# Attention's key blocks moved by 64, with the first block's low part in the free half of its high part

## The chip, the core and the metric

The kernel runs on one core of one Trainium2 chip. TensorE (PE) multiplies matrices: it loads a block of weights of up to 128x128 and streams the columns of the other operand past it, and the result goes to PSUM, which this kernel uses as eight banks of 128 partitions by 512 fp32 columns. ScalarE (ACT), VectorE (DVE) and GpSimd (POOL) do the element work, and SyncE (SP) issues the transfers. The metric is the device time of one execution in microseconds (us), the median of several runs.

## The reference

What is computed is causal attention with a decay bias, and behind it a mixture of four experts, each a two-layer network, weighted by probabilities:

```python
# q, k, v: (4, 8, 576, 64); s: (4, 8, 576)
scores = q @ k^T / 8 ; cum = cumsum(max(s, 0))
scores += min(-(cum[i] - cum[j]), 0), masked where j > i
attn = softmax(scores) ; a = attn @ v          # per head
x = a as (2304 tokens, 512)
p = domain_probs / sum(domain_probs)
out = sum over e of p[:, e] * (relu(x @ w1[e]) @ w2[e])   # 512 -> 1024 -> 512
```

A head has 576 queries and keys: 4 x 128 + 64.

## The kernel before

**Precision.** Most products are split: an operand is written as a high part, which the ACT engine rounds to fp32r, and a low part, the rest, which DVE or POOL subtracts; the products high x high, high x low and low x high are summed in PSUM.

**Attention in visits.** `VISITS` (lines 30 and 31) lists the work. The first eight visits take tiles 0, 1 and 2 of the eight heads of the first batch, the next eight their tiles 3 and 4, and 24 visits the five tiles of each remaining head. Query tile m holds the queries `rows(m)`: tile 0 the first 64, tile m the 128 from 128m - 64 on. Tile m needs the keys 0 to 128m + 64. In the 24 five-tile visits, tile 0 of two heads is done together by `pair_rows`.

For each tile the steps are: scores into a PSUM bank (lines 745 and 748), row maximum with the mask on DVE (line 759), exponential on ACT (line 767), the reciprocal of the sum on DVE (line 775), the normalisation on POOL, ACT or DVE (line 461 or 459), the transposition on PE (line 794), which turns a block of 128 queries by 128 keys so that keys lie on partitions, the high part out of PSUM into `aTh` on ACT (line 466), and the low part on DVE into `aTl` (line 823). When a visit's tiles are through, one run of matmuls with V (line 844) sums over all key blocks, first those of `aTh`, then those of `aTl`. V's high and low part stand side by side in the weights.

**Key blocks.** Block n holds the keys 128n to 128n + 127, block 4 only 64 real ones. Queries and key blocks are thus out of step by 64: a tile m reaches only half into its last block. In the visits behind the first eight, block 4 has no low part of its own. Its unused upper 64 partitions in `aTh` take it (line 826), and V's block 4 holds the last 64 rows twice. The transpositions of tile 4 are in two groups, blocks 0 and 1 in one PSUM bank and blocks 2 to 4 in another (line 783).

**Weights and moving operand of a transposition.** In line 794 the attention block is the weight operand, the identity `idn` the moving one.

**The order.** A planner (`Sched.run`) simulates the engines when the program is built, with costs such as `t_pe` and `t_dve`, priorities and lags, and writes one fixed order for each engine. Attention has the priority. Where PE has nothing of it, the planner puts in matmuls of expert 0 (lines 945 and 960, "fill-in" below) and, early on, dummy matmuls (line 486). What of expert 0 is left follows behind attention, and then come the other experts' products (line 1302), which run from some 400 us to the end.

Of the kernel before, what the change touches and what calls it, by code (L numbers as in the profile page):

```python
# [11 lines left out]
F32 = mybir.dt.float32  # L12
F32R = mybir.dt.float32r
AF = mybir.ActivationFunctionType
ALU = mybir.AluOpType
# [4 lines left out]
B, NH, S, D = 4, 8, 576, 64  # L20
BH = B * NH
E, DM, F = 4, 512, 1024
NT = B * S
P = 128
NC = 5
# [30 lines left out]
    return (0, 64) if m == 0 else (128 * m - 64, 128 * m + 64)  # L56


def fcs_of(tiles):
    return range(KF // 2, KF) if tiles[0] >= PAIRS[LG][0][0] else range(KF)  # L60


def t_pe(n):
    return max(n / 2.4 + 13.5, 110)
# [10 lines left out]
def t_dve(n):  # L75
    return n / 0.96 + 70
# [26 lines left out]
DSLACK = 1100  # L103
T_DSLACK = 15000
T_LAG = 200
S_LAG = 50
PSUM_POOLS = ("S", "T", "X", "mo", "pv")
NWARM = 7
# [30 lines left out]
PT = 0  # L139
PE_ = 0  # L140
# [192 lines left out]
                now = min(later)  # L333


def body(ctx, tc, qk, qkv0, vp, s, dp, w1, w1s, w2, w2s, out):
    nc = tc.nc
    sch = Sched()
    const = ctx.enter_context(tc.tile_pool(name="const", bufs=1))
# [10 lines left out]
    idn = apool.tile([P, P], F32, name="idn")  # L350
# [44 lines left out]
    mo = [b[1] for b in sch.pools["mo"]]  # L395
# [15 lines left out]
    aTh = apool.tile([P, 512 + 5 * 640], F32R, name="aTh")  # L411
    aTl = apool.tile([P, 512 + 5 * 640], F32R, name="aTl")
# [37 lines left out]
    tok = sch.tok  # L450
# [35 lines left out]
        nc.tensor.matmul(b[1][:, 0:256], ones_bf[:, 0:128], ones_bf[:, 0:256], start=True, stop=True)  # L486
        return 110

    for _ in range(NWARM):
        nc.tensor.matmul(mo[1], ones_bf[:, 0:128], ones_bf, start=True, stop=True)  # L490
    nc.vector.memset(warm, 0.0)
    nc.gpsimd.memset(ones, 1.0)
    nc.gpsimd.memset(minus, -1.0)
# [160 lines left out]
    for j, (h, ms) in enumerate(VISITS):  # L654
# [12 lines left out]
        if first:  # L667
            ld = sch.add({"SP": 700}, lambda e, j=j, h=h, ext=ext: nc.sync.dma_start(
                out=AB(j, F32)[0:64, :, 0:ext], in_=qk[h, :, 0:ext].rearrange("(c d) n -> d c n", c=2)),
                prio=base - 1500, take=[("AB", j)], seq="AB", xfer=128 * ext * 4)  # L670
            ldv = sch.add({"SP": 450}, lambda e, j=j, h=h, nb=nb, o=o: nc.sync.dma_start(out=tok[f"vz{h % 2}", j][:, :, o:o + 64], in_=vp[h][:, 0:nb]),
                          prio=base - 1300, take=[(f"vz{h % 2}", j)], seq=f"vz{h % 2}", xfer=nb * 128 * 64 * 4)
        else:
            if pq:
                def f(e, j=j, h=h, ext=ext, q0=q0):
                    nc.sync.dma_start(out=AB(j, F32)[0:64, 1, 0:ext], in_=qk[h, 64:128, 0:ext])
                    nc.sync.dma_start(out=AB(j, F32)[0:64, 0, q0:ext], in_=qk[h, 0:64, q0:ext])
                ld = sch.add({"SP": 800}, f, [firstq.get(j - LA)], prio=base - 1500, take=[("AB", j)], seq="AB", xfer=64 * (2 * ext - q0) * 4)
            else:
                ld = sch.add({"SP": 500}, lambda e, j=j, h=h, ext=ext: nc.sync.dma_start(out=tok["raw", j][:, 0:ext], in_=qk[h, :, 0:ext]),  # L680
                             [firstq.get(j - LA)], prio=base - 1500, take=[("raw", j)], seq="raw", xfer=128 * ext * 4)
            ldv = sch.add({"SP": 450}, lambda e, j=j, h=h, nb=nb: nc.sync.dma_start(out=tok["vraw", j][:, 0:nb], in_=vp[h][:, 0:nb]),
                          [firstq.get(j - LV)], prio=base - 1300, take=[("vraw", j)], seq="vraw", xfer=nb * 128 * 64 * 4)
        ldc = None
        if pq:
# [43 lines left out]
        for m in ms[1:] if joint else ms:  # L729
# [50 lines left out]
            nm = sch.add({"POOL": t_pool(bb), "ACT": (bb / 1.2 + 190, D1), "DVE": (t_dve2(bb), D5 if first else D6)}, f, [rc], prio=pr - PN, give=[("sm", c)])  # L780
            nm.both = True

            tp = [list(range(m + 1))] if m < 4 else [[0, 1], [2, 3, 4]]
            prev = None
            for pi, blocks in enumerate(tp):
                lastp = pi == len(tp) - 1
                w0 = 128 * blocks[0]
                w = 128 * len(blocks) if m else 64

                def f(e, m=m, j=j, blocks=blocks, c=c, pi=pi, first=first):  # L790
                    z = tok[f"a{m}", c]
                    t = tok["T", (c, pi)]
                    for k, x in enumerate(blocks[::-1] if not first and tok["par", j] else blocks):
                        nc.tensor.transpose(t[:, 128 * k:128 * k + 128], z[:, 128 * x:128 * x + 128], idn)  # L794
                tt = sch.add({"PE": t_pe(128) * len(blocks)}, f, [nm, prev, par], prio=pr - PT, take=[("T", (c, pi))],
                             give=[(f"a{m}", c)] if lastp else [])
                tt.lag = T_LAG
                prev = tt

                def region(aT, t, n0, n1, m=m, j=j, blocks=blocks, a=a, bb=bb, first=first):  # L800
                    k0 = 128 * (blocks[-1] + 1 - n1 if not first and tok["par", j] else n0 - blocks[0])
                    k = n1 - n0
                    src = t[:, k0:k0 + 128 * k].rearrange("p (k i) -> p k i", k=k)[:, :, 0:bb - a]
                    return src, tok["aTf", j][:, n0:n1, a:bb] if first else aT_blocks(aT, tok["par", j], n0, n1, a, bb)

                two = m == NC - 1 and blocks[-1] == m

                def f(e, c=c, pi=pi, region=region, blocks=blocks):
                    src, dst = region(aTh, tok["T", (c, pi)], blocks[0], blocks[-1] + 1)
                    hi(e, dst, src)  # L810
                eng = {"ACT": t_act(w)}
                if first:
                    eng["DVE"] = (t_dve(w), D4)
                eh = sch.add(eng, f, [tt], prio=pr - PE_, give=[("T", (c, pi))] if first else [])
                if first:
                    evs.append(eh)
                    continue

                def f(e, c=c, pi=pi, region=region, blocks=blocks, two=two, j=j):
                    t = tok["T", (c, pi)]  # L820
                    n0, n1 = blocks[0], blocks[-1] + 1 - two
                    (src, dst), (_, h_) = region(aTl, t, n0, n1), region(aTh, t, n0, n1)
                    nc.vector.tensor_tensor(out=dst, in0=src, in1=h_.bitcast(F32), op=ALU.subtract)  # L823
                    if two:
                        src, h_ = region(aTh, t, n1, n1 + 1)
                        nc.vector.tensor_tensor(out=h_[64:128, :, 64:128], in0=src[0:64, :, 64:128], in1=h_[0:64, :, 64:128].bitcast(F32), op=ALU.subtract)
                evs.append(sch.add({"DVE": t_dve(w) + 95 * two}, f, [eh], prio=pr - PE_, give=[("T", (c, pi))]))

        pk = ("pair", j // 2)
        pvk = ("pv", pk if first else j)  # L830
        ads = []
        for r0, r1 in ((max(cut, q0), ext),):
            mms = [(aT, n, max(r0, 128 * n), r1) for aT in (aTh, aTl)[0:1 if first else 2] for n in range(nb)
                   if max(r0, 128 * n) < r1 and not (aT is aTl and n == NC - 1)]
            bk = pvk

            def f(e, j=j, mms=mms, first=first, bk=bk, o=o, c0=cut):
                t = tok[bk]
                for i, (aT, n, i0, i1) in enumerate(mms):
                    if first:  # L840
                        st, mv = tok[f"vz{j % 2}", j][:, n, :], tok["aTf", j][:, n, i0:i1]
                    else:
                        st, mv = tok["V", j][:, n, :], aT_blocks(aT, tok["par", j], n, n + 1, i0, i1)[:, 0, :]
                    nc.tensor.matmul(t[:, i0 - c0:i1 - c0], st, mv, start=(i == 0 and not (first and o)),  # L844
                                     stop=(i == len(mms) - 1 and (not first or o > 0)))
            cost = sum(t_pe4(w - u) if first else t_pe(w - u) for _, _, u, w in mms)
            v = sch.add({"PE": cost}, f, evs + [v_ready] + ([prev_v] if first and o else []), prio=base + PO,
                        take=[bk] if not (first and o) else [], give=[(f"vz{j % 2}", j), ("aTf", j)] if first else [("V", j), ("par", j)])
            if first:
                ads.append(v)  # L850
                continue

            def f(e, j=j, o=o, r0=r0, r1=r1, pk=pk, bk=bk, c0=cut):
                nc.scalar.activation(tok["xr", pk][o:o + 64, r0:r1], tok[bk][64 - o:128 - o, r0 - c0:r1 - c0], AF.Copy)
            sh = sch.add({"ACT": t_act(r1 - r0)}, f, [v], prio=base + PO + 10, take=[("xr", pk)] if o == 0 else [])

            def f(e, j=j, o=o, r0=r0, r1=r1, pk=pk, bk=bk, c0=cut):
                xr = tok["xr", pk]
                nc.vector.tensor_tensor(out=xr[o:o + 64, r0:r1], in0=tok[bk][o:o + 64, r0 - c0:r1 - c0], in1=xr[o:o + 64, r0:r1], op=ALU.add)
            ads.append(sch.add({"DVE": t_dve(r1 - r0)}, f, [sh], prio=base + PO + 10, give=[bk]))  # L860
            if joint and o:
                ads += pair_product(j, base, [sh] + prev_ad)
# [676 lines left out]
```

## Time and profile before

| | |
|---|---|
| median of 3 runs | 914.79 us (914.31 to 914.81) |
| profiled execution | 914.74 us, its span 913.0 us |
| PE busy | 905.0 us, 99% |
| DVE busy | 705.6 us, 77% |
| ACT busy | 501.3 us, 55% |
| POOL busy | 506.4 us, 55% |
| DMA | 201.34 MB, 221 GB/s on average |

A matmul appears twice in the profile: as a weight load (PEld) and as the matmul (PE). Both overlap with their neighbours, so that the time one takes of PE is read from start to start. The ACT share is an average: while attention runs, until some 260 us, ACT is busy far above it, and after that at about 40%.

### The profile page before, as it was taken

Reading aid. Unit: us, or ns where it says so; the run is one execution under the profiler, and the core shown is the slowest. Engines: PE = TensorE matmul, PEld = TensorE weight load, DVE = VectorE, ACT = ScalarE, POOL = GpSimd, SP = SyncE. Lnnn points to the kernel's source line nnn. Section 1 sums busy time; section 2 is a strip of 40 time slices with the busy share of each in tenths; the row PEclk is TensorE's granted clock in tenths of the full one; section 3 lists DMA queues with packets and bytes.
Section 4 is the critical chain, followed back from the end, with each engine's and each line's share of the span. In section 5 each row is a group of like instructions: output and inputs, shape, how many; then the busy total and the mean of one; then the engine's idle time right before and its main releaser. Section 6 shows DMA issues by size and latency. Waiting matters only on the chain.

```text
span 913.0 us, 16499 instructions
## 1 busy us (share of the span) xinstructions
PE 905.0 (99%) x5566; PEld 879.2 (96%) x5566; DVE 705.6 (77%) x1599; ACT 501.3 (55%) x1129; POOL 506.4 (55%) x528
## 2 busy tenths in 40 slices
PE   9999999999999999999999999999999999999998
PEld 6789999899999999999999999999999999999998
DVE  6878787888861854888787788788877887787886
ACT  6898999999972334435343533444244534444343
POOL 4688787887744891055344624471366317451655
PEclk9999999999999999999999999999999999999999
DMA  6788887879626996984786468746775667756201
GB/s 165 197 246 236 225 229 219 250 194 255 181 94 221 392 382 239 357 286 173 264 286 207 161 219 303 243 158 218 252 260 200 204 215 253 256 205 220 70 18 69
DMA packets 101279, 201.34 MB, mean 221 GB/s; under 512 B 11256, under 2 KB 66620, under 8 KB 101196
## 3 DMA queue, kind: packets, MB, share of 16 engines
q1 hardware_dynamic: 101196, 200.30, 67.2%
q8 instruction: 44, 0.72, 0.3%
q14 instruction: 39, 0.32, 0.1%
HBM read 157.34 MB, written 29.05 MB: 204 GB/s over the span
## 4 chain that ended last, share of the span: by engine, by line
PE 91%; ACT 4%; DVE 2%; POOL 1%; issue 1%; DMA 1%; SPq 0%; ACTq 0%; POOLq 0%
PE pb L1302 52%; PE mo L1302 9%; PE mo L945 6%; PE mo L960 5%; PE pv L844 4%; PE pb L960 3%; PE T L794 3%; PE S L748 2%; PE pb L945 2%; PE S L745 2%; ACT a L767 1%; PE X L794 1%; ACT aTh L466 1%; DMA AB_r<-AB_r 1%; DVE aTl L823 1%
## 5 line engine op out<-in xcount | busy, mean ns | idle before, releaser
L1302 PE MATMUL pb<-x,w1h 128*128 128x384 f32 x1064 | 270.7, 335 | 0.0
L1302 PEld LDWEIGHTS pb<-x,w1h 128*128 128x128 f32 x1064 | 191.5, 188 | 2.0 <-ACT t L1335 1.5
L1302 PE MATMUL pb<-x,w1l 128*128 128x384 f32 x532 | 177.8, 334 | 0.0
L1310 ACT ACTIVATE pb<-pb 128x384 f32<-128x384 f32 x112 | 53.2, 475 | 200.5 <-DVE t L1342 111.8
L453 POOL TENSOR_TENSOR hT_r<-t,hT_r 128x768 fp32r<-128x768 f32 x18 | 34.3, 1903 | 167.8 <-PE pb L1302 139.4
L1302 PE MATMUL pb<-hT_r,w2h 128*128 128x384 f32 x432 | 109.7, 334 | 0.0
L1302 PEld LDWEIGHTS pb<-x,w1l 128*128 128x128 f32 x532 | 99.9, 188 | 0.0
L466 ACT ACTIVATE hT_r<-t 128x768 fp32r<-128x768 f32 x76 | 64.0, 843 | 47.3 <-PE pb L1302 44.3
L767 ACT ACTIVATE a<-a,mx 128x576 f32<-128x576 f32 (+4 forms) x136 | 81.0, 597 | 12.8 <-DVE mx L759 9.6
L1425 DVE TENSOR_TENSOR acc<-pb,acc 128x384 f32<-128x384 f32 x152 | 78.5, 549 | 9.6 <-ACT pb L1310 6.1
L945 PE MATMUL mo<-xg,w1h 128*128 128x384 f32 (+1 forms) x304 | 78.3, 327 | 0.0
L1302 PEld LDWEIGHTS pb<-hT_r,w2h 128*128 128x128 f32 x432 | 78.0, 188 | 0.0
L453 DVE TENSOR_TENSOR hT_r<-t,hT_r 128x768 fp32r<-128x768 f32 x58 | 59.8, 1031 | 23.2 <-ACT hT_r L466 22.7
L461 POOL TENSOR_SCALAR a<-a,sm 128x576 f32<-128x576 f32 (+5 forms) x111 | 60.5, 552 | 28.6 <-DVE sm L775 15.0
L1302 PE MATMUL pb<-xg,w2h 128*128 128x384 f32 x288 | 73.3, 335 | 0.0
L1302 PE MATMUL pb<-hT_r,w2l 128*128 128x384 f32 x216 | 72.2, 334 | 0.0
L1342 DVE TENSOR_TENSOR t<-pb,t 128x384 f32<-128x384 f32 x78 | 39.8, 551 | 38.5 <-ACT t L1335 25.6
L453 POOL TENSOR_TENSOR xg<-t,xg 128x768 fp32r<-128x768 f32 x19 | 42.9, 2259 | 40.8 <-ACT xg L466 40.8
L1070 DVE TENSOR_TENSOR t<-t 128x768 f32<-128x768 f32 (+1 forms) x42 | 65.1, 1555 | 0.1
L823 DVE TENSOR_TENSOR aTl<-T,aTh 128x256 fp32r<-128x256 f32 (+2 forms) x103 | 51.2, 508 | 4.6 <-ACT aTh L466 3.5
L759 DVE CUSTOM_DVE_ANT_0 a<-S,mask 128x448 f32<-128x448 f32 (+4 forms) x107 | 48.1, 456 | 7.5 <-PE S L745 6.1
L945 PEld LDWEIGHTS mo<-xg,w1h 128*128 128x128 f32 x304 | 52.1, 190 | 1.4 <-issue 0.7
(245 smaller groups left out, 2331.1 us busy)
## 6 DMA issues: line engine op xcount, KB each, us to landing
x<-xs_d SPq DMA_DIRECT2D x68, 768.0 KB
x<-x_d SPq DMA_DIRECT2D x55, 768.0 KB
xs_d<-x SPq DMA_DIRECT2D x12, 768.0 KB
osb<-p_d SPq DMA_DIRECT2D x19, 384.0 KB
w1r<-in_w1s_dram SPq DMA_DIRECT2D x7, 1024.0 KB
w2r<-in_w2s_dram SPq DMA_DIRECT2D x7, 1024.0 KB
KK<-AB_r SPq DMA_DIRECT2D x24, 288.0 KB
xg<-x_d SPq DMA_DIRECT2D x16, 384.0 KB
```

What stands on the lines that cost most here:

```text
L453: (nc.gpsimd if e == "POOL" else nc.vector).tensor_tensor(out=out, in0=in0, in1=in1, op=ALU.subtract)
L461: (nc.gpsimd if e == "POOL" else nc.vector).tensor_scalar(out, in_, scale, 1.0 if bias is None else bias, op0=ALU.mult, op1=ALU.mult if bi ...
L466: nc.scalar.activation(out, in_, AF.Copy)
L759: nc.vector.tensor_tensor_reduce(out=z[0:n, j0:j1], in0=tok["S", (c, pi)][0:n, 0:j1 - j0], in1=mask[0:n, 448 - a + j0:448 - a + j1], scale ...
L767: nc.scalar.activation(z[0:n, 0:bb], z[0:n, 0:bb], AF.Exp, bias=tok["mx", c][0:n, k:k + 1], scale=-1.0, accum_out=tok["sm", c][0:n])
L823: nc.vector.tensor_tensor(out=dst, in0=src, in1=h_.bitcast(F32), op=ALU.subtract)
L945: nc.tensor.matmul(t[:, 0:w], wl[q][:, dc, o:o + P], xgt[:, l, dc, 0:w], start=(u == 0), stop=(u == 3 * KD - 1))
L960: nc.tensor.matmul(t[:, 0:w], wl[fc // 2][:, fc % 2, 128 * dt:128 * dt + 128], ht[:, fc, 0:w], start=(u == 0), stop=(u == 3 * len(fcs) - 1))
L1070: (nc.gpsimd if e == "POOL" else nc.vector).tensor_tensor(out=out, in0=in0, in1=in1, op=op)
L1302: nc.tensor.matmul(ts[u], wv[wl][:, k, 128 * u:128 * u + 128], x[xl_][:, k, :], start=start and k == 0 and n == 0, stop=k == 1 and n == 2, ...
L1310: nc.scalar.activation(out[u], in_[u], AF.Copy)
L1425: nc.vector.tensor_tensor(out=d, in0=ts[u], in1=d, op=ALU.add)
```

## The change

For the visits behind the first eight, the key blocks are moved by 64: `keys(n)` gives block n the keys 128n - 64 to 128n + 63, as the query tiles are, and block 0 the first 64. Tile m then needs the blocks 0 to m in full, and it is block 0 that has 64 free partitions.

- The transposition of block 0 takes 72 columns of the attention tile as weights (64 are needed) and writes 72 partitions; it stands last in its group. Tile 4's groups become blocks 1 to 4 in one bank and block 0 in another.
- The low part of block 0 goes to the upper 64 partitions of its high part, for every tile, as a second subtraction (64x128). The other blocks' low parts are one subtraction.
- The matmuls with V have the column ranges that follow; `aTl` has no block 0.
- V comes from a new array `vd`, with the first 64 rows twice, for these visits. The first eight keep `vp`.
- The seven warm-up matmuls at the start write seven PSUM banks instead of one.
- The planner counts a group with block 0 as 40 ns shorter on PE (`T_HALF`) and the low part with two subtractions as 150 ns longer on DVE (`T_TWO`).

```diff
+def keys(n):
+    return (0, 72) if n == 0 else (128 * n - 64, 128 * n + 64)
...
+T_HALF = 40
+T_TWO = 150
...
-    for _ in range(NWARM):
-        nc.tensor.matmul(mo[1], ones_bf[:, 0:128], ones_bf, start=True, stop=True)
+    warmed = [b[1] for p in ("X", "T", "S") for b in sch.pools[p]] + mo
+    for i in range(NWARM):
+        nc.tensor.matmul(warmed[i], ones_bf[:, 0:128], ones_bf, start=True, stop=True)
...
-            ldv = sch.add({"SP": 450}, lambda e, j=j, h=h, nb=nb: nc.sync.dma_start(out=tok["vraw", j][:, 0:nb], in_=vp[h][:, 0:nb]),
+            ldv = sch.add({"SP": 450}, lambda e, j=j, h=h, nb=nb: nc.sync.dma_start(out=tok["vraw", j][:, 0:nb], in_=vd[h][:, 0:nb]),
...
-            tp = [list(range(m + 1))] if m < 4 else [[0, 1], [2, 3, 4]]
+            tp = [list(range(m + 1))] if m < 4 else [[1, 2, 3, 4], [0]]
...
-                    for k, x in enumerate(blocks[::-1] if not first and tok["par", j] else blocks):
-                        nc.tensor.transpose(t[:, 128 * k:128 * k + 128], z[:, 128 * x:128 * x + 128], idn)
-                tt = sch.add({"PE": t_pe(128) * len(blocks)}, f, [nm, prev, par], prio=pr - PT, take=[("T", (c, pi))],
+                    for k, x in sorted(enumerate(blocks[::-1] if not first and tok["par", j] else blocks), key=lambda y: not first and y[1] == 0):
+                        if first:
+                            nc.tensor.transpose(t[:, 128 * k:128 * k + 128], z[:, 128 * x:128 * x + 128], idn)
+                        else:
+                            u, w = keys(x)
+                            nc.tensor.transpose(t[0:w - u, 128 * k:128 * k + 128], z[:, u:w], idn)
+                tt = sch.add({"PE": t_pe(128) * len(blocks) - T_HALF * (not first and blocks[0] == 0)}, f, [nm, prev, par], prio=pr - PT, take=[("T", (c, pi))],
...
-                    n0, n1 = blocks[0], blocks[-1] + 1 - two
-                    (src, dst), (_, h_) = region(aTl, t, n0, n1), region(aTh, t, n0, n1)
-                    nc.vector.tensor_tensor(out=dst, in0=src, in1=h_.bitcast(F32), op=ALU.subtract)
-                    if two:
-                        src, h_ = region(aTh, t, n1, n1 + 1)
-                        nc.vector.tensor_tensor(out=h_[64:128, :, 64:128], in0=src[0:64, :, 64:128], in1=h_[0:64, :, 64:128].bitcast(F32), op=ALU.subtract)
-                evs.append(sch.add({"DVE": t_dve(w) + 95 * two}, f, [eh], prio=pr - PE_, give=[("T", (c, pi))]))
+                    n0, n1 = blocks[0] + zero, blocks[-1] + 1
+                    if n0 < n1:
+                        (src, dst), (_, h_) = region(aTl, t, n0, n1), region(aTh, t, n0, n1)
+                        nc.vector.tensor_tensor(out=dst, in0=src, in1=h_.bitcast(F32), op=ALU.subtract)
+                    if zero:
+                        src, h_ = region(aTh, t, 0, 1)
+                        nc.vector.tensor_tensor(out=h_[64:128], in0=src[0:64], in1=h_[0:64].bitcast(F32), op=ALU.subtract)
+                evs.append(sch.add({"DVE": t_dve(w) + T_TWO * (zero and m < NC - 1)}, f, [eh], prio=pr - PE_, give=[("T", (c, pi))]))
...
-            mms = [(aT, n, max(r0, 128 * n), r1) for aT in (aTh, aTl)[0:1 if first else 2] for n in range(nb)
-                   if max(r0, 128 * n) < r1 and not (aT is aTl and n == NC - 1)]
+            n0 = 128 if first else 64
+            mms = [(aT, n, max(r0, 128 * n + n0 - 128), r1) for aT in (aTh, aTl)[0:1 if first else 2] for n in range(aT is aTl, nb)
+                   if max(r0, 128 * n + n0 - 128) < r1]
...
-    vp = np.ascontiguousarray(vz.reshape(BH, NC, P, D).transpose(0, 2, 1, 3))
+    vp = np.ascontiguousarray(vz.reshape(BH, NC, P, D).transpose(0, 2, 1, 3)[0:NH])
+    vd = np.ascontiguousarray(np.concatenate([v[:, 0:64], v], 1).reshape(BH, NC, P, D).transpose(0, 2, 1, 3))
```

The lines behind the diff's first places have moved: the transposition of line 794 stands in line 804, the low parts of 823 and 826 in 834 and 837, the matmuls with V of 844 in 856, the fill-in of 945 in 957.

The first place is PE, at the tiles 2 and 3 of an early five-tile visit (tiles `a_1_124` and `a_1_126`) and the matmuls with V of the visit ahead of it. `T`, `X`, `S` and `mo` are PSUM banks; a row reads output, moving operand, weights, and the output's partitions by columns. Before:

```order
L945 MATMUL mo_103<-xg,w1h_76 128x256 x2
L844 MATMUL pv_100<-aTh,V_115 128x512
L844 MATMUL pv_100<-aTh,V_115 128x448
L844 MATMUL pv_100<-aTh,V_115 128x320
L844 MATMUL pv_100<-aTh,V_115 128x192
L844 MATMUL pv_100<-aTh,V_115 128x64
L844 MATMUL pv_100<-aTl,V_115 128x512
L844 MATMUL pv_100<-aTl,V_115 128x448
L844 MATMUL pv_100<-aTl,V_115 128x320
L844 MATMUL pv_100<-aTl,V_115 128x192
L794 MATMUL T_98<-idn,a_1_124 128x128 x3
L794 MATMUL X_101<-idn,a_1_126 128x128 x4
```

Now, for the same tiles and V:

```order
L804 MATMUL X_101<-idn,a_1_124 72x128
L957 MATMUL mo_102<-xg,w1l_80 128x256
L804 MATMUL T_99<-idn,a_1_126 128x128 x3
L804 MATMUL T_99<-idn,a_1_126 72x128
L856 MATMUL pv_100<-aTh,V_115 128x512 x2
L856 MATMUL pv_100<-aTh,V_115 128x384
L856 MATMUL pv_100<-aTh,V_115 128x256
L856 MATMUL pv_100<-aTh,V_115 128x128
L856 MATMUL pv_100<-aTl,V_115 128x512
L856 MATMUL pv_100<-aTl,V_115 128x384
L856 MATMUL pv_100<-aTl,V_115 128x256
L856 MATMUL pv_100<-aTl,V_115 128x128
```

The last transposition of each group has 72 output partitions, the matmuls with V have other columns, and the planner has put this run of them behind the next visit's transpositions instead of ahead of them.

The second place is DVE, at the low parts of the tiles 3 and 4 of a five-tile visit. Before:

```order
L823 TENSOR_TENSOR aTl<-T_99,aTh 128x4x128
L823 TENSOR_TENSOR aTl<-T_98,aTh 128x2x128
L823 TENSOR_TENSOR aTl<-X_101,aTh 128x2x128
L826 TENSOR_TENSOR aTh<-X_101,aTh 64x64
L759 ISA a_1_128,mx_140<-S_97,mask,mx_140 128x288
```

Now:

```order
L834 TENSOR_TENSOR aTl<-mo_102,aTh 128x3x128
L837 TENSOR_TENSOR aTh<-mo_102,aTh 64x128
L782 RECIPROCAL sm_146<-sm_146 128x1
L766 ISA a_1_128,mx_140<-S_96,mask,mx_140 128x288
L766 ISA mx_140 128x1
L780 TENSOR_SCALAR sm_148<-sm_148 128x1
L871 TENSOR_TENSOR cx<-pv_100,cx 64x512
L834 TENSOR_TENSOR aTl<-T_99,aTh 128x4x128
L837 TENSOR_TENSOR aTh<-X_101,aTh 64x128
```

Four subtractions stand in both places, 1,088 columns in all before and 1,152 now; each tile has its second, short one, and between the two tiles the planner has put other work.

## Rows read from the trace of the kernel before

**Rows 1.** The page's first part: busy time, share, instructions of the engines.

```profile
PE 905.0 (99%) x5566; PEld 879.2 (96%) x5566; DVE 705.6 (77%) x1599; ACT 501.3 (55%) x1129; POOL 506.4 (55%) x528
```

**Rows 2.** By stretch: length, busy PE PEld DVE ACT POOL (count), clock, DMA share, GB/s.

```profile
40.00:80.00 40.00, 40.00 (x297) 36.63 (x295) 31.63 (x112) 36.42 (x90) 33.48 (x45) 1.00 0.78 226
80.00:120.00 40.00, 39.32 (x303) 37.85 (x302) 32.75 (x136) 37.38 (x108) 32.23 (x59) 1.00 0.90 236
120.00:160.00 40.00, 39.74 (x307) 38.40 (x307) 33.41 (x129) 37.67 (x105) 32.66 (x56) 1.00 0.81 226
160.00:200.00 40.00, 38.85 (x255) 35.41 (x254) 33.87 (x136) 38.12 (x106) 33.56 (x62) 1.00 0.85 236
200.00:240.00 40.00, 40.00 (x267) 37.76 (x268) 32.40 (x132) 35.91 (x100) 31.22 (x53) 1.00 0.82 238
240.00:272.00 32.00, 32.00 (x212) 30.49 (x211) 25.45 (x90) 26.52 (x72) 17.78 (x37) 1.00 0.31 100
...
500.00:600.00 100.00, 100.00 (x577) 99.62 (x577) 78.92 (x121) 42.86 (x76) 47.89 (x29) 1.00 0.65 224
```

**Rows 3.** Waits of PE from 36 to 272 us: total us, times, longest.

```profile
PE T L633 <- DVE aTl L823: 0.9, 1, 0.9
PE X L748 <- DMA AB_r<-AB_r: 0.7, 1, 0.7
```

**Rows 4.** The chain of waits from 200 to 215 us: start, length in us, what.

```profile
201.58 1.48 PE pv L844 x9
203.05 0.33 PE T L794 x3
203.38 0.43 PE X L794 x4
203.82 0.22 PE T L794 x2
```

**Rows 5.** Timeline of PE and PEld just after 202.8 us: start, duration, what.

```profile
202.80 0.25 PE L844 MATMUL pv<-aTl,V 128*128 128x192 f32 x1
202.89 0.38 PE L794 MATMUL T<-idn,a 128*128 128x128 f32 x2
...
202.81 0.23 PEld L794 LDWEIGHTS T<-idn,a 128*128 128x128 f32 x2
```

**Rows 6.** Timeline of PE just after 10.2 us.

```profile
10.31 0.38 PE L794 MATMUL T<-idn,a 128*128 128x128 f32 x2
10.53 0.38 PE L486 MATMUL mo<-const-bfloat16-1.0 128*128 128x256 bf16 x2
```

**Rows 7.** Groups of weight loads by form: busy us, mean ns, idle before.

```profile
L794 PEld LDWEIGHTS T<-idn,a 128*128 128x128 f32 x326 | 38.3, 141 | 5.3 <-issue 1.0 <-DVE aTl L823 0.4 <-DVE a L461 0.4
...
L844 PEld LDWEIGHTS pv<-aTh,V 128*128 128x128 f32 x160 | 26.0, 189 | 1.9
...
L486 PEld LDWEIGHTS <-const-bfloat16-1.0 128*128 128x128 bf16 x27 | 2.8, 103 | 0.8 <-issue 0.6
```

**Rows 8.** Groups of DVE's subtractions by form, 40 to 250 us, same columns.

```profile
L823 DVE TENSOR_TENSOR aTl<-T,aTh 128x256 fp32r<-128x256 f32 x51 | 20.9, 417 | 1.9 <-ACT aTh L466 1.4
...
L823 DVE TENSOR_TENSOR aTl<-T,aTh 128x512 fp32r<-128x512 f32 x20 | 13.7, 687 | 1.5 <-ACT aTh L466 1.2
...
L823 DVE TENSOR_TENSOR aTl<-T,aTh 128x384 fp32r<-128x384 f32 x20 | 11.0, 548 | 0.3
...
L826 DVE TENSOR_TENSOR aTh<-T,aTh 64x64 fp32r<-64x64 f32 x19 | 4.1, 218 | 0.3
...
L621 DVE TENSOR_TENSOR aT<-T,aT 128x128 fp32r<-128x128 f32 x7 | 2.0, 284 | 0.2
```

**Rows 9.** The chain of waits at a two-tile visit and at 256-column fill-in matmuls.

```profile
62.46 1.03 PE pv L844 x9
...
100.49 1.19 PE mo L960 x10
```

**Rows 10.** The transpositions' line: min/median/max ns, first and last start us.

```profile
L794 PE MATMUL X<-idn,a x123: 270/273/328, 11.7 to 268.8; 128*128 128x128 f32 x123
```

More of the change, by code (lines that the diff above doesn't have):

```diff
@@ L333, in run, with body @@
                 now = min(later)
-def body(ctx, tc, qk, qkv0, vp, s, dp, w1, w1s, w2, w2s, out):
+def body(ctx, tc, qk, qkv0, vp, vd, s, dp, w1, w1s, w2, w2s, out):
     nc = tc.nc
@@ L786, in body @@
                 lastp = pi == len(tp) - 1
-                w0 = 128 * blocks[0]
                 w = 128 * len(blocks) if m else 64
@@ L804, in region @@
                     return src, tok["aTf", j][:, n0:n1, a:bb] if first else aT_blocks(aT, tok["par", j], n0, n1, a, bb)
-                two = m == NC - 1 and blocks[-1] == m
                 def f(e, c=c, pi=pi, region=region, blocks=blocks):
@@ L817, in body, with f @@
                     continue
-                def f(e, c=c, pi=pi, region=region, blocks=blocks, two=two, j=j):
+                zero = blocks[0] == 0
+                def f(e, c=c, pi=pi, region=region, blocks=blocks, zero=zero):
                     t = tok["T", (c, pi)]
-                    n0, n1 = blocks[0], blocks[-1] + 1 - two
-                    (src, dst), (_, h_) = region(aTl, t, n0, n1), region(aTh, t, n0, n1)
-                    nc.vector.tensor_tensor(out=dst, in0=src, in1=h_.bitcast(F32), op=ALU.subtract)
-                    if two:
-                        src, h_ = region(aTh, t, n1, n1 + 1)
-                        nc.vector.tensor_tensor(out=h_[64:128, :, 64:128], in0=src[0:64, :, 64:128], in1=h_[0:64, :, 64:128].bitcast(F32), op=ALU.subtract)
-                evs.append(sch.add({"DVE": t_dve(w) + 95 * two}, f, [eh], prio=pr - PE_, give=[("T", (c, pi))]))
+                    n0, n1 = blocks[0] + zero, blocks[-1] + 1
[6 more added lines that the diff above has]
+                evs.append(sch.add({"DVE": t_dve(w) + T_TWO * (zero and m < NC - 1)}, f, [eh], prio=pr - PE_, give=[("T", (c, pi))]))
         pk = ("pair", j // 2)
@@ L1513 @@
     vz[:, :S] = v
-    vz[:, S:] = v[:, S - 64:]
-    vp = np.ascontiguousarray(vz.reshape(BH, NC, P, D).transpose(0, 2, 1, 3))
+    vp = np.ascontiguousarray(vz.reshape(BH, NC, P, D).transpose(0, 2, 1, 3)[0:NH])
+    vd = np.ascontiguousarray(np.concatenate([v[:, 0:64], v], 1).reshape(BH, NC, P, D).transpose(0, 2, 1, 3))
     x = np.stack([k[NH:, :64], k[NH:, :64], q[NH:, :64], v[NH:, :64]], 1).reshape(-1, 2, 4, 64, D)
@@ L1523 @@
     w2 = np.ascontiguousarray(moe_w2.reshape(E, 4, 2, P, DM).transpose(0, 1, 3, 2, 4)).reshape(E, 4, P, 1024)
-    arrays = {"qk": qk, "qkv0": qkv0, "vp": vp, "s": np.ascontiguousarray(s), "dp": dp, "w1": w1[0:1], "w1s": w1s, "w2": w2[0:1], "w2s": w2s}
+    arrays = {"qk": qk, "qkv0": qkv0, "vp": vp, "vd": vd, "s": np.ascontiguousarray(s), "dp": dp, "w1": w1[0:1], "w1s": w1s, "w2": w2[0:1], "w2s": w2s}
     nc = bacc.Bacc("TRN2", target_bir_lowering=False, num_devices=1, dynamic_dma_scratch_size=512)
```

## The prediction, made before the changed kernel was run

> **What bounds the kernel now.** I read the page's first part first: TensorE (PE) is busy for 99% of the span [rows 1]. Busy is not yet bound, so next comes the table by stretch: from 40 to 272 us, where attention and the fill-in matmuls of expert 0 share the engines, PE is idle for 0.68, 0.26 and 1.15 us in the worst three stretches and for nothing in the others; ScalarE (ACT) is busy for 83 to 95%, VectorE (DVE) for 79 to 85%; the granted clock is 1.00, the 2.4 GHz level [rows 2]. The waits of PE in that part are short and few; the longest is 0.9 us, for a low part that DVE writes [rows 3]. So PE's own steps make the time, and what an edit does to the other engines counts only where it makes PE wait. Only the part up to about 272 us is touched: the last 2,723 rows of PE's order, all after the last transposition, are the same in both kernels, and in both 646 of the 1,152 fill-in matmuls (lines 945 and 960) stand ahead of that point and 506 behind it. Whatever attention gains or loses on PE therefore reaches the end of the kernel in full.
>
> How long is one PE step? The reader should look at start-to-start times, not at durations, since neighbours overlap. In the chain of waits nine transpositions in a row take 0.33 + 0.43 + 0.22 = 0.98 us, or 0.109 us each [rows 4]. The nine matmuls with V of one five-tile visit take 1.48 us [rows 4]. A fill-in matmul with 256 columns advances 0.119 us, and one with 384 columns 100.00 / 577 = 0.173 us [rows 2, 9]: 0.424 ns a column and 10 ns fixed.
>
> **The 72-column transposition.** It is the heart of the change: 112 of the 408 transpositions in visits behind the first eight (4 in each of 24 five-tile visits, 2 in each of 8 two-tile visits) load 72 weight columns in place of 128. The moving operand, the identity, keeps its 128 columns. 101 of the 112 stand right behind another short matmul (99 behind a transposition), where a shorter load could show; the other 11 stand behind a fill-in matmul of 0.12 us or more, which hides the load in any case. So the question is whether 0.109 us is the time of the weight load or that of the matmul itself. Two places tell. First: a 192-column matmul of line 844 starts at 202.80 us, and the transposition behind it at 202.89, 0.09 us later, with its load issued at 202.81, at the start of that matmul; and the nine steps that follow are no longer than elsewhere, so nothing is paid back later [rows 4, 5]. A transposition's load of 128 columns is thus done within 0.09 us, less than the step. Second: where a bf16 matmul follows, the two transpositions ahead of it still take 10.53 - 10.31 = 0.22 us, 0.11 each [rows 6], although the load of that matmul is the shortest of all, 103 ns as recorded against 141 for a transposition and 189 for the matmuls of line 844 [rows 7]. Both say that the matmul of the transposition itself, with 128 moving columns, fills the step. I take **no gain: 0 us**. The trace has no load with fewer than 128 columns, so both ends stay open. If the load did set the step and went with its columns, a step would shrink by 0.109 x 56/128 = 0.048 us, 101 times: -4.8 us. If, at the other end, a 72-column one needed two passes of the array where a 128-column one needs one, each would cost 0.109 us more, 112 times: +12.2 us. The rows above are nearest to zero.
>
> The Trainium skill states a rule that gives the other result: "TensorE: Matmul & The Clock Gate", section "LDWEIGHTS (loading the stationary operand)", has a load last as many ns as it has columns, divided by 1.2, which is 107 for 128 columns and 60 for 72; by that estimate the sum would have 101 x 0.047 = 4.7 us less. The trace doesn't bear it out for transpositions: loads of 128 columns are recorded with 103, 141 and 189 ns [rows 7], and the one at 202.81 us was done in 0.09.
>
> **The matmuls with V.** Before, six long ones (512, 448 and 320 columns, twice) make 2560 x 0.424 + 6 x 10 = 1,145 ns, which leaves 0.11 us for each of the three short ones (192, 64, 192). Now there are seven long ones (512 three times, 384 and 256 twice; 2,816 columns: 1,264 ns) and two short ones (128, 128): 1.49 us. That is +0.01 us, 24 times. A two-tile visit goes from 1.03 us [rows 9] with six of 256 columns and three short ones to seven and two: +0.01 to +0.02, 8 times. Together **+0.3 us**, all on the path.
>
> **The low parts on DVE.** A five-tile visit has three subtractions of 128x256 (0.417), one of 128x384 (0.548), one of 128x512 (0.687) and one of 64x64 (0.218): 2.70 us. Now it has 128, 256, 384 and 512 columns (0.284 + 0.417 + 0.548 + 0.687) and four of 64x128; those aren't in the trace and lie between the 64x64 (0.218) and the 128x256 (0.417), nearest to the 128x128 (0.284), which I take: 3.07 us, +0.37 [rows 8]. A two-tile visit gains 0.06. Together 24 x 0.37 + 8 x 0.06 = **+9.3 us of DVE work** (2 to 24 at the ends of that bound), some 4% of the 236 us. It lies beside PE: DVE idles 15 to 21% there [rows 2]. If that cover is gone it costs up to 9.3 us. Queued behind a low part on DVE are the maxima of the next scores and the reciprocals, and for them wait ACT's exponentials and then PE's transpositions. I put 0 into the sum; the part that may show is the second rival.
>
> **The rest.** ACT's high parts keep their columns (1,792 a visit) and their number (five): the last tile's 256 + 384 becomes 512 + 128. V's loads come from another array with the same shape. The seven warm-up matmuls write seven banks in place of one, on the same engine in the same order. The planner's two new costs and the low parts reshuffle the other engines, but the number of normalisations per visit stays. All that is 0, but the reshuffled order can move PE's small waits: those that are idle time sum to 2.1 us from 40 to 272 [rows 2], so I give them 2 us to either side.
>
> **Sum.** The profiled execution took 914.74 us, 1.74 more than its span; the median of the runs is 914.79, the same within 0.05. 914.74 + 0.0 + 0.3 = 915.0; against the median **915.1 us**.
>
> **Rivals.** (1) *The weight load sets the step after all.* For it: 0.109 us is also about what one of the short matmuls with V takes, whatever its columns, so some load limit of that size exists for those. Against it: rows 5 to 7. Time: 915.1 - 4.8 = 910.3 us. If instead the matmul itself shortened with its weight columns, only the 25 that have another transposition behind them would gain, 25 x 0.048 = 1.2 us (913.9): still no change that can be told.
> (2) *DVE turns late.* Place: the two busiest stretches, 120 to 200 us, where it works 84 to 85% [rows 2] and has some nine visits of 8.6 us. If in these the low part, the last thing a visit's matmuls with V and the next use of a T bank wait for, comes later by its whole 0.37 us and no fill-in stands ready, PE pays 9 x 0.37 = 3.3 us: 918.4 us. It decides once the delay exceeds what fill-in matmuls stand between. For it: PE's longest wait is of this kind [rows 3]. Against it: 6 us of idle DVE in each 40.
> (3) *The 72-column matmul takes two passes:* 915.1 + 12.2 = 927.3 us. The Trainium skill, "TensorEngine Tiling (Array Packing)", section "Restrictions and Gotchas", says that column tiling excludes the transpose mode for fp32; it ties that tiling to 64 columns or fewer, and 72 lies above; no run here shows it.
>
> **Chances.** Forecast 0.50 (915.1, own range 913.0 to 917.2: the 2 us of shifted waits), rival 1 0.26, rival 2 0.21, rival 3 0.03. What a measurement of this kernel can tell from no change is about 0.2%, 1.8 us. Of the forecast 0.42 lies within that, 0.04 on each side; of rival 1 0.24 is faster and 0.02 within; of rival 2 0.20 is slower and 0.01 within; rival 3 is slower. So faster 0.28, within 0.45, slower 0.27 (0.04 + 0.20 + 0.03). The range takes in the middles of rivals 1 and 2 and a little beyond, 910.0 to 918.5, and leaves about 0.2 out: the far halves of both, and rival 3.
>
> **What would show it.** Right: runs of transpositions that end in a 72-column one still take 0.11 us a step; the nine matmuls with V take 1.49 us; the last transposition starts within 2 us of where it does now, at 268.8 us [rows 10]; DVE's low parts sum to some 9 us more. Wrong for rival 1: about 0.06 us from a 128-column transposition to the 72-column one behind it, and an attention part that ends 4 to 5 us sooner. Wrong for rival 2: waits of PE for lines 834 and 837 of the changed kernel, several of 0.3 us or more between 120 and 200 us.

## The result, and the profile after

| | before | after |
|---|---|---|
| median of 4 runs | 914.56 us (914.31 to 914.81) | 919.51 us (918.79 to 919.85) |
| profiled execution, its span | 914.74 us, 913.0 us | 919.85 us, 917.8 us |
| last matmul of attention starts at | 275.9 us | 279.2 us |
| from there to the end of the span | 637.1 us | 638.6 us |

The ratio is 1.0053, 95% interval 1.0036 to 1.0071: the change makes the kernel 4.95 us slower. The forecast of 915.1 us was wrong, and 919.51 lies beyond the range's upper end of 918.5. The third and fourth rows say where to look: 3.3 us are lost inside attention and 1.5 us behind it.

The boundary between the two parts is the last transposition of a finished attention result, line 633 before and 640 after. The first fence is the line's row of before, the second that of after (duration min/median/max in ns, first and last start in us):

```profile
L633 PE MATMUL T<-aT,V x18: 221/276/328, 117.5 to 275.9; 128*128 128x128 f32 x18
```

```profile
L640 PE MATMUL T<-aT,V x22: 221/276/328, 101.5 to 279.2; 128*128 128x128 f32 x22
```

The page's first part of after answers to [rows 1]. VectorE (DVE) has gone from 705.6 to 719.0 us, in 45 more instructions. The low parts are 9.8 us of that: their durations sum to 88.5 us in 224 subtractions, and before to 78.7 in 176. The others sum to 1.8 us less than before; the rest of the rise is recorded instructions that overlap less. ACT and POOL are about where they were:

```profile
PE 910.8 (99%) x5566; PEld 879.6 (96%) x5566; DVE 719.0 (78%) x1644; ACT 500.6 (55%) x1127; POOL 509.3 (55%) x533
```

The stretches of after from 120 us on, with the columns of [rows 2]:

```profile
120.00:160.00 40.00, 39.44 (x291) 36.49 (x290) 36.49 (x146) 35.79 (x103) 33.81 (x57) 1.00 0.82 233
160.00:200.00 40.00, 39.34 (x260) 36.01 (x259) 34.90 (x135) 38.05 (x105) 31.61 (x59) 1.00 0.78 220
200.00:240.00 40.00, 39.79 (x264) 36.72 (x264) 35.86 (x139) 37.57 (x104) 32.69 (x57) 1.00 0.83 238
240.00:272.00 32.00, 31.91 (x209) 29.18 (x208) 27.64 (x106) 27.29 (x75) 19.33 (x40) 1.00 0.34 104
```

Busy PE hardly moves: recorded matmuls overlap (in [rows 5] a transposition starts 0.09 us into a matmul that lasts 0.25), so that one may start later without an idle gap. From 120 to 200 us PE starts 291 + 260 = 551 matmuls where it started 307 + 255 = 562, though not the same ones. DVE is busy for 86 to 91% where it was busy for 80 to 85%.

One engine that waits for DVE is ACT. These are the exponentials that wait for a row maximum from 40 to 272 us (total us, times, longest), before and then after:

```profile
ACT a L767 <- DVE mx L759: 6.2, 14, 1.0
```

```profile
ACT a L774 <- DVE mx L766: 10.5, 18, 1.3
```

The page also follows one chain of work back from the kernel's end, each step to what released it. These are its shares by engine, before and then after:

```profile
PE 91%; ACT 4%; DVE 2%; POOL 1%; issue 1%; DMA 1%; SPq 0%; ACTq 0%; POOLq 0%
```

```profile
PE 87%; DVE 6%; ACT 2%; DMA 2%; issue 1%; SPq 0%; POOL 0%; DVEq 0%; ACTq 0%; POOLq 0%
```

The steps of PE itself are about as they were. In the chain of waits of after, a five-tile visit's nine matmuls with V take 1.47 us, and a transposition with 72 weight columns (the row with `X`) takes 0.11, like each of the four ahead of it:

```profile
205.28 1.47 PE pv L856 x9
...
208.09 0.44 PE T L804 x4
208.53 0.11 PE X L804
```

DVE's low parts, by form, from 40 to 250 us; [rows 8] are those of before:

```profile
L837 DVE TENSOR_TENSOR aTh<-T,aTh 64x128 fp32r<-64x128 f32 x63 | 17.9, 284 | 1.1
...
L834 DVE TENSOR_TENSOR aTl<-T,aTh 128x128 fp32r<-128x128 f32 x14 | 4.0, 286 | 0.9 <-ACT aTh L472 0.9
```

A subtraction of 128 columns takes as long on 64 partitions (0.284 us) as on 128 (0.286); on 64 partitions with 64 columns it took 0.218 [rows 8].

### The profile page after: what moved, and what is told of

It is laid out like the page before. It is cut to its first block, busy times and chain, and to the rows that moved or that the text cites. A ratio compares the mean times of both kernels' runs of the same rounds, so it can differ in the third digit from the quotient of the medians.

```text
span 917.8 us, 16558 instructions
## 1 busy us (share of the span) xinstructions
PE 910.8 (99%) x5566; PEld 879.6 (96%) x5566; DVE 719.0 (78%) x1644; ACT 500.6 (55%) x1127; POOL 509.3 (55%) x533
## 4 chain that ended last, share of the span: by engine, by line
PE 87%; DVE 6%; ACT 2%; DMA 2%; issue 1%; SPq 0%; POOL 0%; DVEq 0%; ACTq 0%; POOLq 0%
PE pb L1314 52%; PE mo L1314 9%; PE mo L957 5%; PE mo L972 5%; PE pv L856 4%; PE T L804 3%; PE S L755 2%; PE pb L972 2%; PE pb L957 2%; DVE a L766 1%; DVE aTl L834 1%; DMA osb<-p_d 1%; ACT a L774 1%; DVE aTh L837 1%; PE S L752 1%
## 5 line engine op out<-in xcount | busy, mean ns | idle before, releaser
L774 ACT ACTIVATE a<-a,mx 128x448 f32<-128x448 f32 (+4 forms) x136 | 81.3, 599 | 16.5 <-DVE mx L766 14.5
L957 PE MATMUL mo<-xg,w1h 128*128 128x384 f32 (+1 forms) x304 | 75.7, 324 | 0.4 <-DVE mx L766 0.2
L467 POOL TENSOR_SCALAR a<-a,sm 128x320 f32<-128x320 f32 (+5 forms) x106 | 58.0, 552 | 32.0 <-DVE sm L782 18.4
L1314 PEld LDWEIGHTS pb<-xg,w2h 128*128 128x128 f32 x288 | 51.9, 188 | 0.3 <-ACT pb L1322 0.2
```

The lines of the kernel that those rows point to most:

```text
L467: (nc.gpsimd if e == "POOL" else nc.vector).tensor_scalar(out, in_, scale, 1.0 if bias is None else bias, op0=ALU.mult, op1=ALU.mult if bi ...
L774: nc.scalar.activation(z[0:n, 0:bb], z[0:n, 0:bb], AF.Exp, bias=tok["mx", c][0:n, k:k + 1], scale=-1.0, accum_out=tok["sm", c][0:n])
L957: nc.tensor.matmul(t[:, 0:w], wl[q][:, dc, o:o + P], xgt[:, l, dc, 0:w], start=(u == 0), stop=(u == 3 * KD - 1))
L1314: nc.tensor.matmul(ts[u], wv[wl][:, k, 128 * u:128 * u + 128], x[xl_][:, k, :], start=start and k == 0 and n == 0, stop=k == 1 and n == 2, ...
```

## Experiments: which part of the change costs the time

Three theories could explain the 3.3 us. By the first, DVE has too much work: its results come later and PE waits. By the second, the order that the planner wrote with its new prices is worse for the same work. That the transposition has become slower is the third.

**The transposition's columns.** All 128 columns, in the changed kernel:

```diff
-    return (0, 72) if n == 0 else (128 * n - 64, 128 * n + 64)
+    return (0, 128) if n == 0 else (128 * n - 64, 128 * n + 64)
```

> The changed kernel with 128 weight columns in the transpositions of block 0 in place of 72; every engine has the same order. If the transposition's own matmul fills its step, as the trace of the changed kernel has it (0.109 us from a 128-column one to the 72-column one behind it), the time stays within 1 us of the changed kernel's 919.5. If the shorter load does save some 0.048 us each, unseen, the time rises by 4 to 5 us, to 924.

919.82 us (918.24 to 920.13), ratio to before 1.0047 [1.0035, 1.0060], attention's last matmul at 279.6 us. Against the changed kernel's 919.51 us, 128 weight columns in place of 72 make no difference that can be measured.

**DVE's added work, taken away in full.** The second subtraction is left out, so that the low part of block 0 is missing:

```diff
-                    if zero:
-                        src, h_ = region(aTh, t, 0, 1)
-                        nc.vector.tensor_tensor(out=h_[64:128], in0=src[0:64], in1=h_[0:64].bitcast(F32), op=ALU.subtract)
```

> The changed kernel without the subtraction that writes block 0's low part (left out of the computation; 112 instructions of 0.284 us on VectorE, 31.8 us, so that it has some 22 us less than the kernel before); every other instruction stands where it stood. If VectorE's added work is what makes TensorE wait, the 3.0 us of added waits in attention go and more with them: 914 to 916.5, with 1.1 to 1.4 us of the rest being the later load of the probabilities behind attention. If the order is the cause and not the work: 918 to 920.

910.27 us (910.17 to 910.80), ratio 0.9948 [0.9936, 0.9961]: 9.2 us less than the changed kernel, and 4.5 less than the kernel before in the same series (914.80). Attention's last matmul is at 271.7 us:

```profile
L640 PE MATMUL T<-aT,V x22: 221/274/327, 100.7 to 271.7; 128*128 128x128 f32 x22
```

It is more than was expected. The edit takes 112 x 0.284 = 31.8 us off DVE, some 22 more than the change had added. So DVE's work already cost time before the change, if the new order by itself is no better than the old; the next run shows that it isn't. ACT's wait for the maxima falls with it, to 2.9 us in 7 waits.

**DVE's work as it was before, in the changed kernel's order.** The second subtraction is left out in 32 of 112 places only, 9.1 us, for one tile of each visit. The low parts then sum to 79.4 us, and before the change to 78.7:

```diff
-                    if zero:
+                    if zero and m != (1 if joint else 3):
```

> The changed kernel with 32 of the 112 second subtractions (64x128) left out, so that the low part of block 0 is missing for one tile of each visit behind the first eight. It takes 32 x 0.284 = 9.1 us of work off VectorE, about what the change had added; the order of every other instruction stays. Theory 'it is the amount of VectorE's work': attention ends some 3 us sooner, near where it did before the change (275.9 us), and the time falls to 915 to 916.5. Rival 'it is the order that the planner wrote': attention still ends near 279 us and the time stays within 1 us of 919.5.

915.12 us (914.43 to 916.51), ratio 1.0005 [0.9994, 1.0016]: the whole loss is gone, with the order of all other instructions as it is in the changed kernel.

```profile
L640 PE MATMUL T<-aT,V x22: 221/274/327, 101.3 to 276.0; 128*128 128x128 f32 x22
```

ACT waits for the maxima for 7.8 us where it waits for 10.5 with all subtractions:

```profile
ACT a L774 <- DVE mx L766: 7.8, 13, 1.3
```

DVE's share of the chain falls from 6 to 3%, and PE's rises from 87 to 90.

Both parts come back: attention's last matmul is at 276.0 us (279.2 with all subtractions, 275.9 before), and 913.1 - 276.0 = 637.1 us are left behind it, as before the change.

**More DVE work in the kernel before.** 48 subtractions of 64x64 are added, each a repeat of a piece of a low part, in the old order:

```diff
+                    if joint and m in (1, 3):
+                        nc.vector.tensor_tensor(out=dst[0:64, 0:1, 0:64], in0=src[0:64, 0:1, 0:64], in1=h_[0:64, 0:1, 0:64].bitcast(F32), op=ALU.subtract)
```

> The kernel before with 48 more subtractions of 64x64 on VectorE (two in each five-tile visit, at the tiles 1 and 3, each a repeat of a part of the low part written just before), 48 x 0.218 = 10.5 us, about what the change adds; the order is that of the kernel before. If VectorE's added work is the cause: 917 to 918.5. If the order is the cause: 914.5 to 915.5.

920.91 us (919.85 to 922.53), ratio 1.0066 [1.0053, 1.0080]. 48 x 0.218 = 10.5 us more on DVE make the old kernel 6.1 us slower, more than expected. Its last attention matmul is at 280.9 us, and the part behind attention is the same 637.1 us:

```profile
L633 PE MATMUL T<-aT,V x18: 220/275/328, 117.3 to 280.9; 128*128 128x128 f32 x18
```

DVE's share of the chain is 6% here too. PE itself now waits for an added subtraction (line 825), once for 1.3 us; ACT's wait for the maxima is 8.1 us, and was 6.2:

```profile
PE T L633 <- DVE aTl L825: 1.8, 2, 1.3
```

The runs together give a price for one us of DVE work: 10.5 us added to the old kernel cost 6.1 (0.58 each), 9.1 us taken from the new one bring 4.4 (0.48 each), and the next 22.7 bring 4.85 (0.21 each; 0.23 by the ratios, since these two runs belong to different series). By the intervals of the ratios the first two are the same (0.58 and 0.48, each with 0.1 to 0.2 either way), and the third is lower: the price falls as DVE gets freer, and nowhere in this range is it zero. All of this work stands at the low parts of the visits. Whether DVE work elsewhere, outside that line of steps, would cost as much was not tried.

## Experiments: the order and the part behind attention

**The planner's price alone, in the kernel before.** Groups with block 0 are counted as 40 ns shorter, and nothing else changes:

```diff
-                tt = sch.add({"PE": t_pe(128) * len(blocks)}, f, [nm, prev, par], prio=pr - PT, take=[("T", (c, pi))],
+                tt = sch.add({"PE": t_pe(128) * len(blocks) - 40 * (not first and blocks[0] == 0)}, f, [nm, prev, par], prio=pr - PT, take=[("T", (c, pi))],
```

> The kernel before, whose planner counts a group with block 0 as 40 ns shorter on TensorE, as the changed kernel's does: the same work in another order. If the planner's wrong price of TensorE or the mere shuffling of the order is the cause: 916.5 to 918.5 with TensorE's waits between 40 and 272 us up by 2 to 3 us. If VectorE's work is the cause: 914 to 915.5.

919.24 us (917.14 to 919.41), ratio 1.0039 [1.0026, 1.0052]: about as slow as the changed kernel, without its work, and beyond what either theory expected. PE's waits from 36 to 272 us have not grown (1.5 us, and 2.0 before); the loss stands elsewhere. The order now has 33 more fill-in matmuls of 384 columns inside attention (679 in place of 646), worth 33 x 0.173 = 5.7 us [rows 2]. The last attention matmul, at 279.7 us, is thus 1.9 us early for the work that lies ahead of it. Behind it stand 637.9 us where 637.1 - 5.7 = 631.4 would do: 6.5 us are lost there. The timeline of DVE shows one place. An addition (line 1070) waits 3.22 us for a buffer that POOL still reads, and the low parts of line 951 are queued behind it:

```profile
307.39 2.31 DVE L1070 TENSOR_TENSOR t<-w1r,t 128x512 f32<-128x512 f32 x1 [3.22 <-POOL x L453]
309.62 0.74 DVE L951 SCALAR_TENSOR_TENSOR hT_r<-pb,hT_r 128x256 fp32r<-128x256 f32 x2
```

PE's waits from 272 to 420 us have these low parts alone:

```profile
PE mo L960 <- DVE hT_r L951: 3.1, 2, 1.6
```

**The price put back, in the kernel after.**

```diff
-T_HALF = 40
+T_HALF = 0
```

> The changed kernel with the planner's price of a group with block 0 put back to the price of the others (T_HALF = 0), since a 72-column transposition takes PE as long as any. All work is the same, the order another. Theory 'VectorE's work sets the loss, whatever the order': 918.5 to 920.5. Rival 'the order that follows from the wrong price is the loss': near 915.

930.47 us (928.72 to 931.92), ratio 1.0174 [1.0160, 1.0189]. Neither theory had this. The work is the same; attention's last matmul comes at 283.5 us, 4.3 us later than with the price, and the part behind it takes 926.7 - 283.5 = 643.2 us, 4.6 longer. Inside attention PE's waits for DVE sum to some 4 us, the longest 1.7, where they sum to 1.1 with the price. Behind it PE waits for loads of expert 0's input:

```profile
PE mo L957 <- DMA xg<-x_d: 3.4, 3, 2.7
```

The price of 40 ns is wrong as a duration (a 72-column step is no shorter), but the order that it gives is 11 us better here than the one of the right price. In the old kernel the same price cost 4.4 us. So with a fixed order this full, a planner's price moved the time in both directions, in ways that neither expectation had; which waits each order makes was seen only when it ran.

**What the changed kernel loses behind attention.** The order there is that of before, and 1.5 us are lost. The chain of waits from 285 to 320 us leaves PE at the loads of two blocks of probabilities, and then has runs of 24 and 48 matmuls that take longer than before:

```profile
292.25 9.87 DMA osb<-p_d
...
302.49 1.16 DVE acc L1238 x4
303.65 0.04 issue
303.69 3.14 PE mo L957 x24
306.84 5.76 PE pb L957 x48
312.60 1.32 PE mo L972 x11
313.91 0.01 issue
313.92 5.55 PE mo L972 x37
```

Before, the same piece is PE alone:

```profile
300.27 2.88 PE mo L945 x24
303.15 5.76 PE pb L945 x48
308.91 5.76 PE mo L960 x48
```

The 24 matmuls take 3.14 us in place of 2.88, the 48 take 1.32 + 5.55 = 6.87 in place of 5.76: 1.37 of the 1.5 us. The loads' row on SP is longer than before, 2.97 us where it was 1.66 (before, then after):

```profile
288.79 1.66 SPq L1037 DMA_DIRECT2D osb<-p_d  x2
```

```profile
292.25 2.97 SPq L1049 DMA_DIRECT2D osb<-p_d  x2
```

To test it, these loads are issued ahead of the others:

```diff
+    steps += [(0.0, -2, b_, lambda b_=b_: prob0(b_)) for b_ in (2, 3)]
```

> The changed kernel with two loads of probabilities of expert 0 issued ahead of the other loads at the start of the part behind attention. Nothing inside attention changes. Theory 'the 1.5 us lost behind attention come from these loads landing late, which makes VectorE's additions late and TensorE's matmuls wait for them': the time from attention's end to the end of the kernel falls by 1.3 to 1.6 us, to some 633.4, and the whole to 917.5 to 918.5. Rival 'that loss has another cause': within 0.5 us of 919.5.

918.31 us (918.05 to 919.44), ratio 1.0044 [1.0032, 1.0057]. The part behind attention falls to 916.8 - 279.4 = 637.4 us, 1.2 less. The median is 1.2 us below the changed kernel's; the two intervals overlap, so that the total alone would not show it, but the matmuls concerned run at their old pace:

```profile
303.78 2.88 PE mo L957 x24
306.66 5.76 PE pb L957 x48
312.42 5.76 PE mo L972 x48
```

Why issuing two loads took 2.97 us stays open. In the run with 32 subtractions left out, the same queue in the same order did it in 1.81 us, and nothing was lost behind attention; so the price of 0.48 above includes this loss. Inside attention alone, 9.1 us taken away bring 3.2 (0.35 each), and 10.5 us added to the old kernel cost 5.0 (0.48 each).

**A better kernel?** The price alone had gained inside attention and lost behind it, so its loss was attacked in three runs. First the due times of the steps behind attention were set 5.6 us earlier:

```diff
-T_RAW = (1.5, 20.0)
-T_SUMS = (16.0, 30.0)
-T_W1 = 49.0
-T_BACK = 50.0
+T_RAW = (1.5, 14.4)
+T_SUMS = (10.4, 24.4)
+T_W1 = 43.4
+T_BACK = 44.4
...
-T_PROB = ((20.0, 4), (43.0, 5))
+T_PROB = ((14.4, 4), (37.4, 5))
```

> The kernel before the change with two edits: the planner's price of a group with block 0 at 40 ns less, as in the run of the planner's price alone, and the due times of the steps behind attention 5.6 us earlier, since in that run VectorE's work behind attention stood too late for TensorE. Theory 'the price alone gains 2 us inside attention and loses 6.6 us behind it to those due times': the loss goes wholly or in most part and the time comes to 912.5 to 915.5. Rival 'that loss is VectorE's own lateness at attention's end, whatever the due times': 917 to 919.5.

927.83 us (926.19 to 928.41), ratio 1.0143 [1.0130, 1.0157], above both expected ranges. The wait on DVE is down from 3.1 to 0.3 us, and a worse one has taken its place, for a load of expert 0's input:

```profile
PE mo L945 <- DMA xg<-x_d: 7.3, 1, 7.3
```

Then, with the old times, only the sums of the next weights were set later:

```diff
-T_SUMS = (16.0, 30.0)
+T_SUMS = (20.0, 33.0)
```

> The kernel before the change with the planner's price alone, as in an earlier run, and the sums of the first weights behind attention 4 and 3 us later on VectorE (T_SUMS 20.0 and 33.0 in place of 16.0 and 30.0), so that VectorE's additions don't stand ahead of the subtractions for which TensorE waits. Theory 'the 6.6 us that were lost behind attention come from one addition that waits for a buffer in front of those subtractions': the part from 295 to 345 us loses less than 1.5 us and the whole comes to 912.5 to 914. Rival 'another wait takes its place': 916 to 919.5.

918.40 us (917.53 to 921.34), ratio 1.0045 [1.0029, 1.0060], as the rival had it. PE waits 1.5 us for the low parts where it had waited 3.1, and 1.4 us for input loads, which is new:

```profile
PE mo L960 <- DVE hT_r L951: 1.5, 1, 1.5
PE mo L945 <- DMA xg<-x_d: 1.4, 4, 0.6
```

With `T_SUMS = (24.0, 36.0)`:

> As the run before, with the sums 8 and 6 us later (T_SUMS 24.0 and 36.0). Same theory: 912.5 to 914. Rival 'the sums are then late for the weights of the next expert': above 916.

918.48 us (916.27 to 921.97), ratio 1.0034 [1.0019, 1.0049], again in the rival's range. The low parts cost PE 1.0 us now, and input loads 3.1. That the addition stood in the low parts' way is borne out in part; what it had cost moves on to other waits in the same stretch. No version here that computes every low part beats the kernel before.

## Why the prediction was wrong

**The 72-column transposition: right in the number, its reason not shown.** The step is 0.11 us, and the run with 128 columns takes the same time. Rival 1 falls: the recorded weight loads do get shorter (114 ns for 72 columns, 140 for 128), but the step does not follow. These are groups of weight loads of after:

```profile
L804 PEld LDWEIGHTS T<-idn,a 128*128 128x128 f32 x233 | 27.3, 140 | 4.8 <-issue 1.7 <-DVE aTl L834 0.5 <-POOL sm L780 0.4
...
L804 PEld LDWEIGHTS T<-idn,a 128*72 128x72 f32 x74 | 8.5, 114 | 0.4
```

The Trainium skill's rule ("TensorE: Matmul & The Clock Gate", section "LDWEIGHTS (loading the stationary operand)": columns divided by 1.2, by that estimate 47 ns less for 72 columns than for 128) is a rule on the load. The records have 26 ns less, and none of it shows in the step. Rival 3 falls too: a 72-column transposition takes one step of 0.11 us, not two.

Two readings of the prediction went too far here. That the load of 202.81 us "is thus done within 0.09 us" isn't in the rows: a load of this kind is recorded with 0.14 us [rows 7], so the record ends behind its matmul's start at 202.89. And that the 128 moving columns fill the step isn't shown: a matmul with V of 128 moving columns is followed by a transposition after 0.06 us (the median of 18 places in the trace of after). The runs show that the step does not depend on whether there are 72 or 128 weight columns; what sets its 0.11 us stays open.

**The matmuls with V: right to 0.02 us.** 1.47 us a visit, forecast 1.49. The +0.01 us a visit did not come: the median of the 24 five-tile visits is 1.483 us before and 1.471 after. Of the two short matmuls the last takes 0.06 us up to a transposition behind it, and I had taken 0.11 for each.

**The low parts on DVE: size right, price wrong.** The 64x128 subtraction takes the 0.284 us that I had taken for it, and the low parts grew by 9.8 us in all, forecast 9.3. The step that failed is the overlap: the work "lies beside PE", and so "I put 0 into the sum". Its reason was that DVE idles 15 to 21% of a stretch. The runs that change DVE's work put the term at 0.48 to 0.58 us for each us, 4.5 to 5.4 us for 9.3. Why the idle time is no cover is my reading and not shown by itself: that share is an average over steps; in a visit the maximum, the reciprocals, the low parts and the results stand in one fixed line, and a step that comes 0.28 us later delays those behind it, whatever idle time follows.

**Rival 2: the right cause, by another route.** Its 3.3 us, 0.37 for each of nine visits from 120 to 200 us, equal what was lost inside attention, but that is luck. Counted from start to start of PE's matmuls, with the same length for each kind of step in both traces, some 1.6 us are lost from 120 to 200 us and some 1.5 from 200 us to attention's end; that is an estimate, and grouping the steps otherwise moves it by 1 us. Only about half of the place is borne out; DVE is busy for 86 to 91% in all four stretches from 120 on. Nor is the sign that I had named seen: in the whole of attention PE has one wait of 0.3 us for line 837, and none longer for 834 or 837:

```profile
PE T L640 <- DVE aTh L837: 0.3, 1, 0.3
```

In the old order with more DVE work that sign does appear, with PE's wait of 1.3 us for an added subtraction between 120 and 200 us.

How DVE's delay reaches PE in the changed kernel is not settled. One route is a detour through ACT's exponentials, whose wait for the maxima grew from 6.2 to 10.5 us. It can't be all: in the old order with more DVE work that wait grew by 1.9 us only, and attention lost 5.0. The chain has more of DVE itself (6% in place of 2) and less of ACT (2% in place of 4), but in the run with 128 weight columns, as slow and in the same order, it has 4% of DVE and 4% of DMA, so that one chain is a rough measure. In PE's steps the loss shows as many small gaps.

**The part behind attention: missed.** "Whatever attention gains or loses on PE therefore reaches the end of the kernel in full" held the order to be enough. The order is the same there; the time is 1.5 us longer, and 1.2 of it goes when two late loads are issued earlier. Without this loss the time would have been 918.0, inside the range, but at the end that rival 2 had opened, 2.9 us from the forecast.

**The sign of the last transposition.** It starts at 272.8 us, 4.0 later than before, where I had allowed 2:

```profile
L804 PE MATMUL T<-idn,a x307: 270/272/332, 37.2 to 272.8; 128*128 128x128 f32 x119, 128*72 128x128 f32 x35
```

**Shifted waits of 2 us to either side: too narrow.** The same work under another price of 40 ns took 930.47 in place of 919.51 us. The changed kernel's own order costs about nothing once DVE's work is as before, as the run with 80 of 112 subtractions shows (1.0005); that could not be read from the trace before.

## What to carry to other kernels

Work that is added to an engine isn't free because the engine has idle time on average. Here ACT and DVE were busy for some 80 to 95% beside a full PE, and a us of added DVE work cost about half a us. Before such a term is put at nothing, look at who waits for that engine's other results, here ACT for the maxima. Fewer weight columns brought nothing in steps of 0.11 us. A planner's price, even a wrong one, can move the time more than the edit that it comes with, so an edit and its new order are to be timed apart.

## What the runs showed of the hardware

When PE stood still for a load, its clock fell and stayed low after the load had come. These are stretches of the run with the earlier due times (length, busy PE, PEld, DVE, ACT and POOL with counts, clock, DMA share, GB/s):

```profile
340.00:344.00 4.00, 0.00 (x0) 0.00 (x0) 0.00 (x0) 1.60 (x2) 4.00 (x3) 0.99 1.09 370
344.00:346.00 2.00, 0.00 (x0) 0.00 (x0) 0.00 (x0) 0.00 (x0) 2.00 (x2) 0.50 1.05 388
...
348.00:350.00 2.00, 2.00 (x7) 1.54 (x7) 0.00 (x0) 0.00 (x0) 0.00 (x0) 0.50 1.08 376
350.00:352.00 2.00, 2.00 (x11) 2.00 (x11) 0.43 (x1) 0.49 (x1) 0.15 (x1) 0.81 1.06 431
352.00:354.00 2.00, 2.00 (x14) 2.00 (x13) 0.47 (x2) 0.86 (x2) 1.92 (x2) 1.00 0.93 383
```

PE starts no matmul from 340 to 346 us. The granted clock was 1.00 (2.4 GHz) until some 344 us, 0.50 (1.2 GHz) until past 350, and 1.00 again from 352. From 348 to 350 us PE starts 7 matmuls, from 352 to 354 it starts 14. In the chain of this run the 24 matmuls behind the load take 6.47 us, and the next 24 take 4.17, at the full clock; the wait of 7.3 us thus cost some 2.3 us more:

```profile
346.63 6.47 PE mo L945 x24
353.10 4.17 PE pb L945 x24
```
